# Attention's small products regrouped in the first pass of a two-block kernel

## The chip, the cores and the metric

The kernel runs on one core of a Trainium2 chip. The time is device microseconds (us) of that core for one execution. Before the change the median of three runs is 789.23 us (788.98 to 789.61).

## The reference

Two blocks follow each other. The first is an attention without softmax, per batch and head; the second mixes along the sequence and then along the channels.

```python
kv = np.einsum('bhsd,bhse->bhde', k, v)            # 8 x 8 heads, seq 576, head_dim 64
out = np.einsum('bhsd,bhde->bhse', q, kv)
rms = np.sqrt(np.mean(out * out, axis=-1, keepdims=True) + 1e-06)
x = out / rms * g_norm                             # then (B, S, H*D) = (8, 576, 512)
h = np.maximum(x.transpose(0, 2, 1) @ w_tok1, 0.0) @ w_tok2     # 576 -> 256 -> 576
u = x + h.transpose(0, 2, 1)
result = u + np.maximum(u @ w_ch1, 0.0) @ w_ch2    # 512 -> 1536 -> 512
```

All is float32.

## The kernel before

The kernel has two passes. The first does attention and the mixing along the sequence; the second, from 193.8 us on, does the channel part. Only the first is changed.

The first pass takes the eight batches in four pairs. While one pair is mixed, the next one's attention is computed. So there are five stages, each a list of strings: `start` (attention of pair 0), `middle` (attention of pair 1, mixing of pair 0), two `steady` lists (attention of pair 2 and 3, mixing of pair 1 and 2), and `last` (mixing of pair 3). `play` (L1192) walks through a list and calls the step of each name. Every step emits its instructions at once, and all of them are kept in program order, so the lists are the order of the work on each engine and each queue. A name with a minus sign takes the step from the attention of the pair before. A digit means so many steps of the weight conversion that VectorE and ScalarE do on the side for the second pass.

The steps, with `s` the batch of the pair, `c` a tile pair of 256 sequence rows (0 and 1 of the first batch, 2 and 3 of the second; 4 holds the 64 remaining rows of both), and `t` or `h` a half:

- `kv{s}{h}` (L364): k times v for four heads, 20 matrix products that fill 64 of the array's columns; into a PSUM bank of pool `kv`, two banks. `e{s}{h}` (L379): ScalarE copies them to SBUF (`kvp`).
- `a{c}` (L404, and L418 for `a4`): q times kv, 32 products (16 for `a4`) of 64×64, four of them side by side in the array; into two PSUM banks of pool `o`, which has two.
- `g{c}{h}` (L435): VectorE multiplies a bank by the gain into the tile `x`. `q{c}{h}` (L446): ScalarE squares the bank. `t{c}{h}` (L460): VectorE sums the squares per head.
- `m`, `r`, `i` (L468, L473, L477): mean on VectorE, root on ScalarE, inverse in four VectorE instructions, once for a whole group of tiles. The groups of pairs 1 to 3 are (0, 1) and (2, 3, 4).
- `s`, `d`, `p` with a tile and a half (L493, L500, L504): scale x by the inverse, on ScalarE (eight instructions), VectorE (one) or GpSimd (one).
- `h{s}{t}` (L532): first mixing product of a batch, half of the 256 token features, four full-array products over 512 columns. `hr` (L539): the remaining rows, 64 rows of the array, followed by four ReLU of ScalarE.
- `z{i}` (L550): ScalarE copies x of tile i into a PSUM bank as the seed of the sum. `u{i}` (L556): second mixing product, two full-array products; `u8`, the remaining rows, four products that fill 64 columns. With a seed (i = 2, 4, 6) ScalarE copies the result to x, otherwise VectorE adds it. Odd i and 8 then write x to memory on GpSimd's queue. The banks of `h`, `z` and `u` come from pool `h`, which has four, in turn.
- `x{u}{half}` (L636): four VectorE transposes of finished tiles into a free part of a weight tile, and `b{u}{half}` (L620) their transfer to memory.
- `l`, `lq`, `lr`, `f`: loads of k and v, of q, of q's remainder, of raw weights, on SyncE's queue.

Every matrix product of float32 leaves two records in the profile, so `u0` is a group of 4, `h00` of 8, `kv00` of 40, `a0` of 64, `a4` of 32, `hr` and `u8` of 8. All matrix products have the same line, L133, that of a helper; the groups are told apart by their tiles: `ps_kv`, `ps_o` and `ps_r` for attention, `ps_h` and `ps_u` for the mixing.

Of the kernel before, what the change touches and what calls it, by code (L numbers as in the profile page):

```python
# [11 lines left out]
F32 = mybir.dt.float32  # L12
# [8 lines left out]
def kernel(  # L21
# [33 lines left out]
    P = 128  # L55
    B, S, DM = k.shape
    D = g_norm.shape[0]
# [7 lines left out]
    HP = H // 2  # L65
# [12 lines left out]
    def pool(name, bufs, side="left", stack=ctx, **kw):  # L78
        return stack.enter_context(tc.tile_pool(name=name, bufs=bufs, side=side,
                                                reuse_waits="tile", **kw))  # L80
# [15 lines left out]
    ps = {n: pool(f"ps_{n}", b, "left", psums, space=bass.MemoryType.PSUM)  # L96
          for n, b in (("o", 2), ("kv", 2), ("h", 4))}
# [34 lines left out]
    def matmul(*a, **kw):  # L132
        keep(nc.tensor.matmul(*a, **kw))  # L133
# [220 lines left out]
    def attention(pair, groups):  # L354
# [47 lines left out]
                           rhs=kvp[side][:, hp], start=True, stop=True)  # L402

        def attend(c):  # L404
            o = [ps["o"].tile([P, 2, HP, D], F32, name="ps_o", tag="o") for _ in range(2)]
            side = c // 2
            for t in range(2):
                for hp in range(HP):
                    for n in range(2):
                        for h in range(2):  # L410
                            r = ds(h * D, D)
                            matmul(o[h][ds(n * HF, HF), t, hp],
                                   lhsT=qT[2 * pair + side][r, hp, ds((2 * (c % 2) + t) * P + n * HF, HF)],
                                   rhs=kvp[side][r, hp, :D], start=True, stop=True)
            for h in range(2):
                bank[c, h] = o[h].rearrange("p t k d -> p (t k) d")

        def attend_rem():  # L418
            o = [ps["o"].tile([P, HP, D], F32, name="ps_r", tag="o") for _ in range(2)]
            for hp in range(HP):  # L420
                for side in range(2):
                    for h in range(2):
                        r = ds(h * D, D)
                        matmul(o[h][ds(side * HF, HF), hp], lhsT=q_rest[2 * pair + side][r, hp],
                               rhs=kvp[side][r, hp, :D], start=True, stop=True)
            for h in range(2):
                bank[4, h] = o[h]
# [86 lines left out]
        for c in range(5):  # L514
            if whole:
                steps |= {f"a{c}{t}": do(attend_tile, c, t) if c < 4 else attend_tile_rem
                          for t in range(parts(c))}
            else:
                steps[f"a{c}"] = do(attend, c) if c < 4 else attend_rem
            for h in range(parts(c)):  # L520
                steps |= {f"{n}{c}{h}": do(f, c, h) for n, f in zip("gqt", (gain, square, total))}
            for t in range(1 if c == 4 else 2):
                steps |= {f"{n}{c}{t}": do(f, c, t) for n, f in zip("spd", (scale, scale_pool, scale_vector))}
# [668 lines left out]
    def play(lines, after={}, **stages):  # L1192

        for name in " ".join(lines).split():
            if name.isdigit():
                for _ in range(int(name)):
                    next(stages["rounding"], lambda: None)()
            elif name[0] == "-":  # L1200
                stages["before"][name[1:]]()
            else:
                next(stages[s][name] for s in ("attention", "mixing", "more")
                     if name in stages.get(s, ()))()
# [28 lines left out]
    for block in tok1[2:] + tok2:  # L1233
# [11 lines left out]
        "h010 t21 m2 r2", "a30 g30 q30 i2 p20", "a31 g31 q31 t30", "h011 t31 m3 r3 p21", "a40 i3 p30 g40 q40 p31",  # L1245
        "h012 h013 t40 m4 r4 w21 i4 s40 lq0 l10 l11 lr0 lr1"]
    middle = [
        "kv00 e00 w31 w22 w23 w24", "h10 -lq1 w32 w33 w34", "kv01 e01 w41 w42",
        "h11 w43 w44", "hr l00", "a0 q00 g01 q01 g00 t00 t01", "u0 z2 f0", "u1 l01",
        "a1 q10 g11 q11 g10 t10 t11 m0 r0 lq0", "u2 i0", "kv10 e10 z4 d00", "u3 s01", "kv11 e11",  # L1250
        "u4 z6 f1", "a2 q20 g21 q21 g20 s10", "u5 t20 t21 f2", "a4 q40 g41 q41 g40 lr0 lr1 1", "u6 t40 t41 1 l10",
        "a3 q30 g31 q31 g30 lq1 d11", "u7 t30 t31 m2 r2 1 i2 p20 p21 s30", "u8 1 l11 d31"]
    steady = [[
        "kv00 kv01 e00 e01 1 -d40 f3", "h00 1 x00", "h01 1 f4 b00", "a0 q00 g01 q01 g00 l00 1",
        "h10 t00 t01 1 x01", "h11 l01 1 x10 b01", "hr 1 x11 z2 f5 f6", "a1 q10 g11 q11 g10 lq0", "kv10 kv11 e10 e11 t10 t11 m0 r0",
        "u0 i0 1", "u1 1 d00 l10", "u2 s01 z4 1 f7", "a2 q20 g21 q21 g20", "u3 s10 t20 t21",
        "u4 z6 l11", "a4 q40 g41 q41 g40 lr0 lr1 1", "u5 d11 t40 t41 1", "a3 q30 g31 q31 g30 lq1",
        "u6 t30 t31 m2 r2 i2 d20 p21 s30", "u7 1 d31 1", "u8 1 b10 b11"], [
        "kv00 kv01 e00 e01 1 -d40 f8", "h00 1 x20", "h01 1 f9", "a0 q00 g01 q01 g00",
        "h10 t00 t01 1 x21", "h11 1", "hr 1 z2 f10", "a1 q10 g11 q11 g10", "kv10 kv11 e10 e11 t10 t11 m0 r0",  # L1260
        "u0 i0 1", "u1 1 d00 f11", "u2 s01 z4 1", "a2 q20 g21 q21 g20", "u3 s10 t20 t21",
        "u4 z6 1 f12", "a4 q40 g41 q41 g40", "u5 d11 t40 t41 1", "a3 q30 g31 q31 g30",
        "u6 t30 t31 m2 r2 i2 d20 p21 s30", "u7 1 d31 b20 b21", "u8 f13"]]

    attentions = [attention(0, ((0,), (1,), (2,), (3,), (4,)))]
    attentions += [attention(p, ((0, 1), (2, 3, 4))) for p in range(1, B // 2)]

    mixings = [token_mixing(p, (2, 4, 6)) for p in range(B // 2 - 1)]
    mixings.append(token_mixing(B // 2 - 1, range(2, 9), (0, 1)))
# [15 lines left out]
    play(middle, attention=attentions[1], mixing=mixings[0], before=attentions[0],  # L1285
         more=more, rounding=rounding)
    for n in range(1, B // 2 - 1):
        play(steady[n - 1], attention=attentions[n + 1], mixing=mixings[n], before=attentions[n],
             more=more, rounding=rounding)


# [5 lines left out]
    for i in range(2):  # L1297
# [2 lines left out]
    woven = fill[0][:4] + fill[1] + fill[0][4:]  # L1300

    last = [
        "h00 2 -d40 2 o0", "h01 2 o1", "h10 2 o3", "h11 2 o2", "hr z2 1 o4", "u0 z3 1 c0", "u1 z4 1 c1 o5", "u2 z5 c2",
        "u3 z6 1 c3 o6", "u4 z7 1", "u5 z8 1", "u6 1 s0", "u7 s1 s2", "u8 s3 s4"]
    parts1 = [f for o in ORDER1 for f in split(1, o)]
    more = {f"c{i}": f for i, f in enumerate(t_sums(lambda n: uT[0][:, SB[n]]))}
# [97 lines left out]
```

## Time and profile before

| | |
|---|---|
| median of three runs | 789.23 us |
| the profiled execution's own time | 788.88 us |
| its span | 787.1 us |
| TensorE busy | 774.4 us, 98% |
| VectorE busy | 612.9 us, 78% |
| ScalarE busy | 265.4 us, 34% |
| GpSimd busy | 78.3 us, 10% |
| middle | 39.79 to 76.41 us |
| first steady stage | 76.41 to 119.21 us |
| second steady stage | 119.21 to 162.11 us |
| last stage | 162.11 to 193.76 us |

The stages are read from the starts of their first matrix products. In a row of the profile, PE is TensorE, DVE VectorE, ACT ScalarE, POOL GpSimd, SP SyncE. A row of the listing in order of time has the start, the length, engine, line, operation, output and input tiles, the shape and how many were merged; in brackets, idle time before it and what ended it. The ends of matrix products are modelled, so the text takes differences of starts.

### The profile page before, as it was taken

The page shows a single profiled execution, that of the slowest core. Times are in us where ns is not written, and L with a number is a line of the kernel's source. Part 1 is how long each engine was busy: PE and PEld are TensorE (multiplying, and loading weights), DVE is VectorE, ACT ScalarE, POOL GpSimd, SP SyncE. Part 2 cuts the span into 40 slices and gives each one's busy share as a digit, 9 for nine tenths or more (in the row PEclk, how much of TensorE's full clock was granted, in tenths as well). Part 3 has the DMA queues.
Part 4 walks back from the last instruction along what each step waited for, and adds up shares of the span by engine and source line. Part 5 has one row for each costly group of instructions (what it writes and reads, how often), then busy time and mean ns, then how long its engine had stood idle before and what let it go on. Part 6 is the DMA issues. An engine that isn't in the chain of part 4 may idle for free.

```text
span 787.1 us, 14853 instructions
## 1 busy us (share of the span) xinstructions
PE 774.4 (98%) x5832; PEld 652.6 (83%) x5832; DVE 612.9 (78%) x906; ACT 265.4 (34%) x513; POOL 78.3 (10%) x91
## 2 busy tenths in 40 slices
PE   6999999999999999999999999999999999999998
PEld 5655555544888888999988899998889999889998
DVE  2666887796776868988778889776898885787977
ACT  2356564846110133511133242123352113325211
POOL 1211212122410000010100001010000101000111
PEclk9999999999999999999999999999999999999999
DMA  9999999587699795599897579889559889655864
GB/s 295 327 334 371 361 371 344 212 268 282 235 292 337 269 339 148 154 309 205 246 236 231 151 218 272 247 203 290 148 158 283 206 222 230 200 153 151 200 173 91
DMA packets 132614, 192.12 MB, mean 244 GB/s; under 512 B 13633, under 2 KB 92225, under 8 KB 132545
## 3 DMA queue, kind: packets, MB, share of 16 engines
q1 hardware_dynamic: 115984, 167.54, 68.1%
q0 software_dynamic: 14656, 22.02, 13.7%
q10 hardware_dynamic: 1904, 1.61, 0.7%
q8 instruction: 46, 0.75, 0.4%
q14 instruction: 24, 0.19, 0.1%
HBM read 138.31 MB, written 52.82 MB: 243 GB/s over the span
## 4 chain that ended last, share of the span: by engine, by line
PE 95%; DVE 2%; ACT 1%; DMA 1%; issue 0%; SPq 0%; ACTq 0%
PE ps_d L133 28%; PE ps_b L133 19%; PE ps_a L133 19%; PE ps_h L133 8%; PE ps_u L133 8%; PE ps_v L133 5%; PE ps_c L133 3%; PE ps_kv L133 2%; PE ps_w L133 2%; PE ps_o L133 2%; DMA raw<-in_moe_w_tok_dram 1%; ACT x L498 1%; DVE x L444 0%; DVE ms L465 0%; PE ps_j L133 0%
## 5 line engine op out<-in xcount | busy, mean ns | idle before, releaser
L133 PE MATMUL ps_d<-ui,w 128*128 128x256 f32 x504 | 118.6, 379 | 0.0
L133 PEld LDWEIGHTS ps_d<-ui,w 128*128 128x128 f32 x504 | 95.1, 190 | 12.8 <-DVE v L124 0.2
L130 ACT COPY ps_d<-ps_a 128x768 f32<-128x768 f32 (+1 forms) x56 | 32.0, 571 | 215.6 <-PE ps_a L133 215.6
L124 DVE TENSOR_TENSOR v<-v,v 128x1536 f32<-128x1536 f32 (+2 forms) x70 | 103.5, 1483 | 0.3
L133 PE MATMUL ps_b<-w,sv 128*128 128x128 f32 x672 | 84.7, 276 | 0.0
L133 PE MATMUL ps_a<-w,v 128*128 128x128 f32 x672 | 84.2, 275 | 0.0
L133 PEld LDWEIGHTS ps_a<-w,v 128*128 128x128 f32 x672 | 79.9, 192 | 0.2
L133 PEld LDWEIGHTS ps_b<-w,sv 128*128 128x128 f32 x672 | 79.5, 192 | 0.2
L133 PE MATMUL ps_u<-h,w_tok 128*128 128x512 f32 (+1 forms) x160 | 67.2, 606 | 0.2
L133 PE MATMUL ps_d<-w,v 128*128 128x128 f32 x528 | 66.3, 275 | 0.0
L133 PE MATMUL ps_h<-x,w_tok 128*128 128x512 f32 (+1 forms) x160 | 65.5, 603 | 0.7 <-ACT x L498 0.7
L133 PEld LDWEIGHTS ps_d<-w,v 128*128 128x128 f32 x528 | 62.7, 192 | 0.3
L127 ACT ACTIVATE v<-v 128x768 f32<-128x768 f32 (+1 forms) x54 | 42.6, 821 | 55.1 <-DVE v L124 55.1
L133 PE MATMUL ps_d<-w,sv 128*128 128x128 f32 x480 | 60.1, 275 | 0.0
L133 PEld LDWEIGHTS ps_d<-w,sv 128*128 128x128 f32 x480 | 57.1, 192 | 0.2
L133 PEld LDWEIGHTS ps_h<-x,w_tok 128*128 128x128 f32 (+1 forms) x160 | 26.1, 189 | 32.7 <-issue 29.0
L1121 POOL DMA_DIRECT2D out_dram<-us x11 | 14.1, 1278 | 379.3 <-ACT us L130 347.4
L133 PEld LDWEIGHTS ps_u<-h,w_tok 128*128 128x128 f32 (+1 forms) x160 | 24.8, 179 | 31.0 <-issue 25.6
L133 PE MATMUL ps_a<-uT,w 128*128 128x256 f32 x192 | 46.7, 379 | 0.0
L444 DVE TENSOR_TENSOR x<-ps_o,g_sb 128x512 f32<-128x512 f32 x32 | 21.6, 687 | 28.6 <-PE ps_o L133 23.3
L133 PE MATMUL ps_b<-ui,w 128*128 128x256 f32 x168 | 40.8, 379 | 0.0
L133 PEld LDWEIGHTS ps_a<-uT,w 128*128 128x128 f32 x192 | 36.3, 190 | 4.8
(145 smaller groups left out, 1216.2 us busy)
## 6 DMA issues: line engine op xcount, KB each, us to landing
w<-parts SPq DMA_DIRECT2D x168, 384.0 KB, 4.1
w<-parts SPq DMA_DIRECT2D x56, 192.0 KB, 3.4
uT<-blocks SPq DMA_DIRECT2D x36, 256.0 KB, 5.7
k_in<-in_k_dram SPq DMA_DIRECT2D x16, 512.0 KB, 8.7
qT<-in_q_dram SPq DMA_DIRECT2D x8, 1024.0 KB, 9.2
out_dram<-x POOLq DMA_DIRECT2D x16, 512.0 KB, 6.1
v_in<-in_v_dram SPq DMA_DIRECT2D x14, 512.0 KB, 8.8
raw<-in_moe_w_ch_dram SPq DMA_DIRECT2D x8, 768.0 KB, 10.4
```

What stands on the lines that cost most here:

```text
L124: keep(engine.tensor_tensor(out=o, in0=a, in1=b, op=op))
L127: keep(nc.scalar.activation(o, a, AF.Relu))
L130: keep(nc.scalar.copy(o, a))
L133: keep(nc.tensor.matmul(*a, **kw))
L444: keep(nc.vector.tensor_mul(x, bank[c, h], g_sb.to_broadcast([P, number(c), D])))
L498: keep(nc.scalar.activation(x[:, k, h], x[:, k, h], AF.Copy, scale=inv[:, k, h]))
L1121: keep(nc.gpsimd.dma_start(to.rearrange("t p e -> p t e"), a, accum_op=ALU.add))
```

## The change

- `a0` and `a4` put their results into the banks of pool `kv` instead of pool `o`.
- `a3` with all that follows it (its squares, gains, sums, `d31`, `s30`) goes to the start of the next stage, and so do `u8` and the load `lq1`. In the second steady stage `a3` and `u8` stand at the end, and `i3`, `d31`, `s30` in the last stage.
- The groups of the statistics become (0, 1), (2, 4) and (3,).
- Within the stages kv steps stand side by side, `a3` with `a0`, `a2` with `a4`; in `middle` also `a0` with `a1`. Seeds (`z`), transposes (`x`) and conversion steps are put at other places in the lists.

```diff
         def attend(c):
-            o = [ps["o"].tile([P, 2, HP, D], F32, name="ps_o", tag="o") for _ in range(2)]
+            n = "o" if c else "kv"
+            o = [ps[n].tile([P, 2, HP, D], F32, name="ps_o", tag=n) for _ in range(2)]
...
         def attend_rem():
-            o = [ps["o"].tile([P, HP, D], F32, name="ps_r", tag="o") for _ in range(2)]
+            o = [ps["kv"].tile([P, HP, D], F32, name="ps_r", tag="kv") for _ in range(2)]
...
     middle = [
-        "kv00 e00 w31 w22 w23 w24", "h10 -lq1 w32 w33 w34", "kv01 e01 w41 w42",
-        "h11 w43 w44", "hr l00", "a0 q00 g01 q01 g00 t00 t01", "u0 z2 f0", "u1 l01",
-        "a1 q10 g11 q11 g10 t10 t11 m0 r0 lq0", "u2 i0", "kv10 e10 z4 d00", "u3 s01", "kv11 e11",
-        "u4 z6 f1", "a2 q20 g21 q21 g20 s10", "u5 t20 t21 f2", "a4 q40 g41 q41 g40 lr0 lr1 1", "u6 t40 t41 1 l10",
-        "a3 q30 g31 q31 g30 lq1 d11", "u7 t30 t31 m2 r2 1 i2 p20 p21 s30", "u8 1 l11 d31"]
+        "kv00 kv01 e00 e01 w31 w22 w23 w24", "h10 -lq1 w32 w33 w34", "h11 w41 w42 w43 w44", "hr l00",
+        "a0 q00 g01 q01 g00 t00 t01", "a1 q10 g11 q11 g10 t10 t11 m0 r0 l01 lq0", "u0 z2 f0", "u1 z4 i0 d00",
+        "u2 s01", "kv10 kv11 e10 e11 x00", "u3 s10 d11 f1", "u4 z6 l10", "a2 q20 g21 q21 g20",
+        "a4 q40 t20 g41 q41 t21 g40 lr0 lr1 1", "u5 t40 t41 m2 r2 f2", "u6 1 i2 p20 p21 l11", "u7 1 1"]
     steady = [[
-        "kv00 kv01 e00 e01 1 -d40 f3", "h00 1 x00", "h01 1 f4 b00", "a0 q00 g01 q01 g00 l00 1",
-        "h10 t00 t01 1 x01", "h11 l01 1 x10 b01", "hr 1 x11 z2 f5 f6", "a1 q10 g11 q11 g10 lq0", "kv10 kv11 e10 e11 t10 t11 m0 r0",
-        "u0 i0 1", "u1 1 d00 l10", "u2 s01 z4 1 f7", "a2 q20 g21 q21 g20", "u3 s10 t20 t21",
-        "u4 z6 l11", "a4 q40 g41 q41 g40 lr0 lr1 1", "u5 d11 t40 t41 1", "a3 q30 g31 q31 g30 lq1",
-        "u6 t30 t31 m2 r2 i2 d20 p21 s30", "u7 1 d31 1", "u8 1 b10 b11"], [
...
+        "kv00 kv01 e00 e01 -d40 f3", "-u8", "-a3 -q30 -g31 -q31 -g30 -t30 -t31 -m3 -r3",
+        "a0 q00 g01 q01 g00 -i3 -d31 -s30 t00 t01 -lq1 l00", "h00 b00 1 1", "h01 f4 x01 1", "h10 1 l01 b01 x10",
+        "h11 1 x11 1", "hr z2 f5 f6", "a1 q10 g11 q11 g10 lq0", "kv10 kv11 e10 e11 t10 t11 m0 r0", "u0 i0 1",
+        "u1 z4 1 d00 l10", "u2 s01 1 f7", "a2 q20 g21 q21 g20", "a4 q40 t20 g41 q41 t21 g40 lr0 lr1", "u3 s10 l11",
+        "u4 z6 t40 t41 m2 r2 d11", "u5 1 i2 d20 p21 1", "u6 1 x20", "u7 1 1 b10 b11"], [
+        "kv00 kv01 e00 e01 -d40 f8", "-u8", "-a3 -q30 -g31 -q31 -g30 -t30 -t31 -m3 -r3",
+        "a0 q00 g01 q01 g00 -i3 -d31 -s30 t00 t01 -lq1", "h00 1 1", "h01 f9 x21 1", "h10 1", "h11 1 1", "hr z2 f10",
+        "a1 q10 g11 q11 g10", "kv10 kv11 e10 e11 t10 t11 m0 r0", "u0 i0 1", "u1 z4 1 d00 f11", "u2 s01 1",
+        "a2 q20 g21 q21 g20", "a4 q40 t20 g41 q41 t21 g40", "u3 s10", "u4 z6 t40 t41 m2 r2 d11 1 f12",
+        "u5 1 i2 d20 p21", "u6 1 b20 b21", "u7", "a3 q30 g31 q31 g30", "u8 t30 t31 m3 r3 f13"]]
...
-    attentions += [attention(p, ((0, 1), (2, 3, 4))) for p in range(1, B // 2)]
+    attentions += [attention(p, ((0, 1), (2, 4), (3,))) for p in range(1, B // 2)]
...
-        play(steady[n - 1], attention=attentions[n + 1], mixing=mixings[n], before=attentions[n],
+        play(steady[n - 1], attention=attentions[n + 1], mixing=mixings[n], before=attentions[n] | {"u8": mixings[n - 1]["u8"]},
...
-        "h00 2 -d40 2 o0", "h01 2 o1", "h10 2 o3", "h11 2 o2", "hr z2 1 o4", "u0 z3 1 c0", "u1 z4 1 c1 o5", "u2 z5 c2",
+        "h00 -i3 -d31 -s30 2 -d40 2 o0", "h01 2 o1", "h10 2 o3", "h11 2 o2", "hr z2 1 o4", "u0 z3 1 c0", "u1 z4 1 c1 o5", "u2 z5 c2",
```

The second steady list of before is the first with other loads, transposes and transfers; it ends with "u7 1 d31 b20 b21", "u8 f13".

## The prediction

> **What bounds the kernel now.** I read the page first, then TensorE in order of time, then ScalarE in order of time.
>
> ```profile
> PE 774.4 (98%) x5832; PEld 652.6 (83%) x5832; DVE 612.9 (78%) x906; ACT 265.4 (34%) x513; POOL 78.3 (10%) x91
> ...
> PE 95%; DVE 2%; ACT 1%; DMA 1%; issue 0%; SPq 0%; ACTq 0%
> ```
>
> TensorE is busy 98% of the span and 95% of the chain that ended last. So a microsecond put into or taken out of TensorE's order moves the end by a microsecond, as long as nobody else becomes late. Next, TensorE in order of time (start, length with modelled end, group; I use differences of starts):
>
> ```profile
> 52.69 3.70 PE L133 MATMUL ps_u<-h,w_tok 128*128 128x512 f32 x8
> 56.32 1.16 PE L133 MATMUL ps_o<-kvp,qT 64*64 64x64 f32 x64
> 57.41 1.98 PE L133 MATMUL ps_u<-h,w_tok 128*128 128x512 f32 x4
> 59.33 1.39 PE L133 MATMUL ps_kv<-v_in,k_in 128*64 128x64 f32 x40
> 60.64 1.98 PE L133 MATMUL ps_u<-h,w_tok 128*128 128x512 f32 x4
> ...
> 97.07 2.55 PE L133 MATMUL ps_kv<-v_in,k_in 128*64 128x64 f32 x80
> 99.55 5.42 PE L133 MATMUL ps_u<-h,w_tok 128*128 128x512 f32 x12
> 104.90 1.16 PE L133 MATMUL ps_o<-kvp,qT 64*64 64x64 f32 x64
> 105.99 4.09 PE L133 MATMUL ps_u<-h,w_tok 128*128 128x512 f32 x8
> 110.01 0.69 PE L133 MATMUL ps_r<-kvp,qR 64*64 64x64 f32 x32
> ```
>
> Full-array runs of 4, 8 and 12 records between tiled ones take 1.91, 3.63 and 5.35: 0.4293 per record plus 0.197, the price of the two edges. One kv step takes 1.31, two side by side 2.48, not 2.63; so a kv step is 1.166 plus edges of 0.05 in and 0.10 out. An attention step takes 1.09 = 0.933 + 0.159, the remainder 0.62 = 0.466 + 0.159. The run of 8 at 105.99 takes 4.02 against 3.63: u4 waited 0.39 there, 0.28 until its seed was in the bank and 0.10 for starting again. ScalarE in the same stretch shows why, and what the change will meet:
>
> ```profile
> 105.06 0.58 ACT L130 COPY x<-ps_u 128x512 f32<-128x512 f32 x1 [2.42 <-PE ps_u L133]
> 105.54 2.02 ACT L498 ACTIVATE x<-x,inv 128x64 f32<-128x64 f32 x8
> 107.46 0.58 ACT L130 COPY ps_u<-x 128x512 f32<-128x512 f32 x1
> 107.98 1.06 ACT L448 ACTIVATE sq<-ps_o 128x512 f32<-128x512 f32 x2
> 108.94 2.01 ACT L498 ACTIVATE x<-x,inv 128x64 f32<-128x64 f32 x8
> 110.85 0.57 ACT L130 COPY x<-ps_u 128x512 f32<-128x512 f32 x1
> 111.31 0.59 ACT L130 COPY ps_u<-x 128x512 f32<-128x512 f32 x1
> ```
>
> ScalarE runs gapless from copying u2 out (105.06), through s01, z4, the squares of tile 2 and s10, to copying u4 out and seeding z6 (111.31), in just the order of the step lists. TensorE's u4 waits for z4 in that queue.
>
> **The skill.** "TensorEngine Tiling (Array Packing)", Key Properties: changing the tiling mode, not just the tile, drains TensorE. The trace agrees: an edge costs 0.05 to 0.10, two products of one form none. "TensorE: Matmul & The Clock Gate", the section on the 16 sub-arrays: ScalarE and VectorE take their queues strictly in order. The listing agrees; my waits rest on this. "PSUM — Partial Sum Buffer", the section on bank collisions: two engines may not use one bank at once, two readers included. Here the square of the second bank starts only after its gain (58.36 after 57.58+0.69).
>
> **The edges.** From middle's first kv product at 39.79 to the last stage's first product at 162.11 are 122.32 us. Tiled with the prices above, the new order without any wait is:
>
> - middle: kv kv 2.48, h10 h11 7.07, hr 1.92, a0 a1 2.03, u0–u2 5.35, kv kv 2.48, u3 u4 3.63, a2 a4 1.56, u5–u7 5.35: 31.87.
> - first steady stage: kv kv 2.38, u8 1.82 (the same form as kv, so one edge less), a3 a0 2.03, h00–h11 13.93, hr 1.92, a1 1.09, kv kv 2.48, u0–u2 5.35, a2 a4 1.56, u3–u7 8.78: 41.34.
> - second: the same, a3 1.09 and u8 1.87 at its end: 44.30.
>
> Sum 117.51, which is 4.81 less. Of this 1.43 are waits of before that go: a3 for the o bank (0.31 at 71.64, 0.17 and 0.18 inside the later a3) and u4 for z4 (0.385 twice). The edges proper give 3.38.
>
> **New wait in middle, at u2.** z2 now stands behind the whole of tile 1, r0 (the square root) included; r0 needs m0, which needs t11. Tensor order: u0 starts 53.28, so u2 is wanted at 53.28+0.10+8×0.4293 = 56.82. hr ends at 51.25; in before the last relu ended 1.67 after hr, so 52.93 here. q00 then runs 52.86–53.46, and VectorE steps on at its usual spacing (0.6 each): g00 53.49, t00 54.10, t01 54.69, g11 55.28, g10 55.89, t10 56.49, t11 57.08–57.76, m0 to 57.97, r0 58.00–58.24, z2 58.14–58.75. With 0.05 to TensorE, u2 starts 58.80: 1.98 late, 2.08 with the restart. Behind r0 on ScalarE only z2 and z4 wait.
>
> **New wait in both steady stages, at u6.** z4 moves up and is on time. z6 still follows u4, but a2 and a4 now go before u3, so all their squares stand ahead of it while TensorE has no attention left to spend time on. From u2's end, T: copy u2 T+0.25, s01 +0.73 (8 at 0.239 = 1.92), q20 +2.66, g20 after it +3.29, t20 +3.90, g41 +4.50–4.91, q41 +5.00, s10 +5.27 (1.92), copy u4 +7.19, z6 +7.66–8.24, u6 +8.30. TensorE wants u6 at T + 1.65 (a2 a4) + 5.26 (u3–u5) = T+6.91: 1.39 late, 1.49 with the restart.
> In the second stage the conversion count puts the ScalarE half of a block between s01 and q20: 18 conversion steps are done before the stage, six more by h11, and u0, u1, u2 bring the 25th to 27th; the 27th starts channel block 9, of the 1024 form (1.15+1.12, some 2.07 in a row). All behind it shifts by that: 3.46, with restart 3.56.
>
> **What else moves.** A third group of statistics: mean, root and inverse for c=3, some 1.05 us of VectorE and 0.23 of ScalarE per pair (by the 16-column rows near 39.5: 0.18, 0.25, 0.18, 0.18, 0.25 and 0.22). a3's squares, sums, d31 and s30 and u8's add go to the next stage's start. h10 needs s30 at its third product, 15.1 us into the stage; a3 ends at 5.1, then g31, g30, t30, t31, m3, r3, g01, g00, i3 bring s30 to its end at about 13.0. Two microseconds of cover; a later s30 would be paid one to one. POOL's u8 stores (0.58, 0.60, 0.55) move with u8, and its X buffer is wanted by g40 only 25 us later. lq1 (1 MB, 9.2 to landing) passes SP's f3 or f8 and follows a3; a2 wants it 25 us on. It costs nothing unless 15 late, and blocks b10, b11 come free of the wait they had behind it. x00 (1.4 of VectorE) enters middle, x20 the first steady stage; VectorE was busy 23.72 of 36.60 in middle, so the gaps carry it. kv10 finds a0's banks free 6 us earlier. In the last stage t30, t31, m3, i3, d31 are new on VectorE, 3.1 us; it stood idle 7.21 before ps_v, so they fit.
> An unseen quantity is the edge from kv's 128×64 form to 64×64 through u8; taken like others at 0.15, its bounds are the smallest edge seen, 0.05, and a whole pair of them, 0.35, so −0.2 to +0.4 over the two stages.
> After 162 TensorE shows no wait over 0.11 us, so the shift goes through to the end.
>
> **Sum.** −3.38 −1.43 +2.08 +1.49 +3.56 = +2.3 us. Against the profiled execution's own 788.88 (span 787.1) this gives 791.2; the median is 0.35 above it, so I predict 791.5. A measurement here tells about 0.2%, 1.6 us, from no change.
>
> **Rivals.**
>
> 1. *Smaller waits, within 0.2%.* If block 9's conversion does not fall ahead of q20, the second stage waits like the first: 2.3−2.07 = +0.2, 789.5. For it: conversion steps may slip when VectorE is late. Against: both queues are written out in order, so the conversion can only slip as a whole. 0.22.
> 2. *Faster: no wait at z6.* If ScalarE reaches z6 before u5 ends, the 1.49 and 3.56 vanish and 5.05 less gives 786.4. The place is the stretch copy u2 to z6; it decides if this stretch is 1.4 shorter in one stage and 3.5 in the other. Against: 0.239 per scale and 0.5 per square are in every row. 0.08.
> 3. *Slower still: h10 waits for s30.* VectorE beside POOL's scaling is slow: the conversion's last step took 1.48 instead of 0.92 at 163.54, and "SBUF — State Buffer", Who interferes with whom, describes such blocking. If that and a late raw block eat the two microseconds of cover and one more in each stage, +2 gives 793.5. 0.12.
>
> My forecast has 0.58, its own range 790.6 to 792.3. Faster: rival 2 and a sliver, 0.09. Within: rival 1 with the low end of the forecast, 0.24. Slower: 0.67. The range reaches over rival 1 and most of rival 3: 789.2 to 793.4.
>
> **What would show it.** Right: ps_u waits near 56.8 for 2 us until a seed copy that follows a root; one near 111.7 of about 1.4 and one near 154.4 of about 3.5, each ended by a seed copy; first product of the last stage at about 164.4 instead of 162.11; kv and attention groups starting 2.48 and 2.03 apart. Wrong: seeds copied before the root or before s10; h10 waiting for s30; waits of TensorE after 162.

## The result, and the profile after

The median rises from 789.16 us to 797.40 us (four runs each: 788.98 to 789.61 before, 795.93 to 797.78 after). The ratio is 1.0099, with a 95% interval of 1.0086 to 1.0113. The forecast of 791.5 had the direction, but only 2.3 of the 8.2 us, and its range ended at 793.4.

The head of the page and the chain that ended last, of the kernel after:

```profile
PE 774.4 (97%) x5832; PEld 653.9 (82%) x5832; DVE 616.4 (78%) x921; ACT 267.0 (34%) x516; POOL 77.9 (10%) x91
...
PE 88%; DMA 5%; DVE 2%; ACT 2%; issue 1%; SPq 1%; ACTq 0%; DVEq 0%
```

The number of products is the same, and so is TensorE's busy time, in a span of 795.2 us instead of 787.1. Nearly all of the 8.1 us more stand in the first pass. Its stages now start at 39.87 (middle), 74.19, 118.82 (steady) and 169.85 (last), and the second pass at 201.50. The last stage takes 31.65 as before. It starts 7.74 later than before, of which 0.08 were there at the start of middle. The other 0.36 of the 8.1 come in the second pass and were not looked into.

That DMA has 5% of the chain instead of the 1% of before is not 4% of lost time. Followed back, the chain leaves TensorE at the second kv step of middle, which waits 0.19 us for v, and runs through transfers and their issue from there to the start. In the kernel before, it goes through the engines in that stretch.

The list of TensorE's waits between 39 and 195 us has the names (us in total, times, longest; short waits are left out of it):

```profile
PE ps_u L133 <- ACT ps_u L130: 6.2, 3, 3.2
PE ps_o L133 <- issue: 2.8, 2, 1.5
PE ps_kv L133 <- DMA v_in<-in_v_dram: 0.2, 1, 0.2
```

The first row was forecast: three groups of products (u2, and u6 twice) that wait for a seed which ScalarE copies into PSUM. The other two were not. In the second row, "issue" says that TensorE waited for nothing that the profile shows. TensorE in order of time gives the places:

```profile
53.76 3.70 PE L133 MATMUL ps_u<-h,w_tok 128*128 128x512 f32 x8
59.26 1.98 PE L133 MATMUL ps_u<-h,w_tok 128*128 128x512 f32 x4 [1.79 <-ACT ps_u L130]
...
78.39 2.09 PE L133 MATMUL ps_o<-kvp,qT 64*64 64x64 f32 x126
81.98 0.33 PE L133 MATMUL ps_o<-kvp,qT 64*64 64x64 f32 x2 [1.51 <-issue]
...
108.57 5.42 PE L133 MATMUL ps_u<-h,w_tok 128*128 128x512 f32 x12
115.19 3.70 PE L133 MATMUL ps_u<-h,w_tok 128*128 128x512 f32 x8 [1.20 <-ACT ps_u L130]
...
123.02 1.74 PE L133 MATMUL ps_o<-kvp,qT 64*64 64x64 f32 x103
126.06 0.58 PE L133 MATMUL ps_o<-kvp,qT 64*64 64x64 f32 x25 [1.31 <-issue]
...
152.90 5.42 PE L133 MATMUL ps_u<-h,w_tok 128*128 128x512 f32 x12
161.56 5.40 PE L133 MATMUL ps_u<-h,w_tok 128*128 128x512 f32 x8 [3.24 <-ACT ps_u L130]
```

- u0 to u2 take 7.41 instead of 5.35: u2's wait, +2.06. u3 to u7 of the first steady stage take 10.25 instead of 8.78: u6's wait, +1.47.
- a3 and a0 side by side take 3.85 and 3.56 instead of 2.03. TensorE stops two records (one product) before the end of a0 in one stage and 25 records before it in the other, in the middle of a group whose other products run.
- In the second steady stage u3 to u7 take 13.99. The wait before u6 is 3.51 of the surplus. The rest follows it: u6 and u7 start 5.33 before the next group, where eight such records otherwise take 3.63. That is 1.70 more, and the row's 5.40 against 3.70 in the first stage shows it too.

The view of stretches has what TensorE was given in that one (stretch, length, busy time of TensorE, its weight loads, VectorE, ScalarE and GpSimd, granted clock, DMA share, GB/s):

```profile
161.60:166.90 5.30, 5.30 (x10) 2.00 (x10) 4.94 (x9) 1.85 (x4) 2.28 (x2) 0.68 0.82 247
```

The granted clock is 0.68 on average here and 1.00 in the stretch before. Taken more finely, it is 0.50 from 161.92 to 165.33, so for 3.41 us, and 1.00 around that. The records in it come 0.85 us apart instead of 0.43; half of 3.41 are the 1.70 that were lost.

ScalarE in order of time shows both kinds of seed as the prediction has them, z2 behind the root and z6 behind squares and scaling:

```profile
58.49 0.23 ACT L476 ACTIVATE root<-ms 128x32 f32<-128x32 f32 x1 [1.34 <-DVE ms L471]
58.62 1.09 ACT L130 COPY ps_u<-x 128x512 f32<-128x512 f32 x2
...
153.91 1.11 ACT L163 ACTIVATE w_ch<-raw 128x1024 f32<-128x1024 f32 x1
154.93 1.13 ACT L166 ACTIVATE raw<-raw 128x1024 uint32<-128x1024 uint32 x1
155.96 1.05 ACT L449 ACTIVATE sq<-ps_o 128x512 f32<-128x512 f32 x2
...
158.55 2.01 ACT L499 ACTIVATE x<-x,inv 128x64 f32<-128x64 f32 x8
160.46 0.57 ACT L130 COPY x<-ps_u 128x512 f32<-128x512 f32 x1
160.93 0.59 ACT L130 COPY ps_u<-x 128x512 f32<-128x512 f32 x1
```

Put together, from starts of matrix products (us, in the profiled execution):

| term | forecast | measured |
|---|---|---|
| edges | −3.38 | −3.38 |
| waits of before that go | −1.43 | −1.43 |
| u2 waits for z2 | +2.08 | +2.06 |
| u6 waits for z6, first steady stage | +1.49 | +1.47 |
| u6 waits for z6, second steady stage | +3.56 | +3.51 |
| u6 and u7 after it at a lower clock | 0 | +1.70 |
| pauses between a3 and the end of a0 | 0 | +1.83, +1.53 |
| kv01 waits for v | 0 | +0.41 |
| start of middle | 0 | +0.08 |
| sum, to the last stage | +2.3 | +7.8 (7.74 by the stage starts) |

### The profile page after: what moved, and what is told of

It reads as the page before. It is cut to its first block, busy times and chain, and to the rows that moved or that the text cites. A ratio compares the mean times of both kernels' runs of the same rounds, so it can differ in the third digit from the quotient of the medians.

```text
span 795.2 us, 14874 instructions
## 1 busy us (share of the span) xinstructions
PE 774.4 (97%) x5832; PEld 653.9 (82%) x5832; DVE 616.4 (78%) x921; ACT 267.0 (34%) x516; POOL 77.9 (10%) x91
## 4 chain that ended last, share of the span: by engine, by line
PE 88%; DMA 5%; DVE 2%; ACT 2%; issue 1%; SPq 1%; ACTq 0%; DVEq 0%
PE ps_d L133 27%; PE ps_b L133 18%; PE ps_a L133 18%; PE ps_h L133 7%; PE ps_u L133 7%; PE ps_v L133 5%; DMA v_in<-in_v_dram 3%; PE ps_c L133 3%; PE ps_w L133 2%; PE ps_kv L133 2%; PE ps_o L133 1%; ACT x L499 1%; DMA raw<-in_moe_w_tok_dram 1%; SPq L121 1%; DMA xt<-out_dram 1%
```

## The theory and its rivals

What had to be explained were the pauses in a3–a0 (3.36) and the lower clock (1.70).

**Instructions.** The trace lists TensorE's instruction queue among the DMA queues: 46 packets, 0.75 MB, 16.3 KB each. TensorE leaves 5832 records of products and as many of weight loads, some 254 per packet. In the stretch from 79 to 82.5 us the view of transfers has exactly one such packet:

```profile
q8 instruction: 1, 0.02, 1.8%
```

The trace has it from 79.79 to 80.77; TensorE goes on at 81.98. The second starts at 123.75, and TensorE goes on at 126.06. Counted over TensorE's records, the two pauses stand before instruction 1985 and 3009, which are 1024 or four times 256 apart. So it looks as if instructions come in blocks of 256, one per packet, and TensorE gets to the end of a block before the next one is there. kv kv u8 a3 a0 are 160 + 16 + 256 = 432 instructions in 6.2 us; the block before 1985 would have been done in 2.82 us. In the kernel before, the shortest block of the first pass from middle on lasts 7.95. "Runtime: NRT & Kernel Launch", Instruction fetch mechanics, in the Trainium skill has the same sizes: blocks of 16 KiB, 256 instructions, the next one fetched while the current one runs. It calls the cost mostly hidden; at these two places it isn't, and the measurement decides.

The rival: a0 or a3 waits for a bank, for q or for kv in a way that the profile doesn't name.

**The clock.** "TensorE: Matmul & The Clock Gate", What's actually happening, says that the array falls to half its rate after an idle window of about 3.4 us. The gap between two records was 3.84 us here. After u2's wait, a gap of 2.39, there was nothing of the kind. The rival: what the records read or what runs beside them makes them slow.

## The experiments

All times are medians; the kernel before stood between 788.95 and 789.18 in the four groups of runs.

### z2 ahead of tile 1

```diff
-        "a0 q00 g01 q01 g00 t00 t01", "a1 q10 ... m0 r0 l01 lq0", "u0 z2 f0", ...
+        "a0 q00 g01 q01 g00 z2 t00 t01", "a1 q10 ... m0 r0 l01 lq0", "u0 f0", ...
```

> In the middle stage the seed z2 follows a0's square of the first bank instead of tile 1's root. Theory: u2's pause of 2.06 us in the middle stage is nothing but the seed's place in ScalarE's queue; the pause goes, TensorE is 2.06 us earlier from there on, 797.2 - 2.06 = 795.1. Rival: u2 waits for something else too (the PSUM bank that the seed goes into, the shared x), then the pause stays near 2 us and the time within 0.5 us of 797.2.

Measured: 795.08 (791.47 to 797.20). ScalarE in order of time copies the seed 4.8 us earlier than in the kernel after, directly behind a0's squares:

```profile
52.89 1.09 ACT L449 ACTIVATE sq<-ps_o 128x512 f32<-128x512 f32 x2
53.86 0.61 ACT L130 COPY ps_u<-x 128x512 f32<-128x512 f32 x1
```

u0 to u2 take 5.35 again, and the first steady stage starts 2.38 earlier (2.06 from u2, most of the rest from v's wait, which isn't there in this execution). The rival falls. The median agrees less well than it looks, for the runs spread over 5.7 us: in the profiled one, of 797.20, a lower clock also follows the first a3–a0 pause (2.04 here) and costs 1.70 us, and the one behind z6 lasts longer (6.83 us, which cost 3.08 instead of 1.70).

### z6 ahead of s01

```diff
-        ... "u2 s01 1 f7", ... "u4 z6 t40 t41 m2 r2 d11", ...
+        ... "u2 z6 s01 1 f7", ... "u4 t40 t41 m2 r2 d11", ...
```

The second steady list has the same edit.

> In both steady stages the seed z6 follows u2 instead of u4. Theory: the pauses at u6 (1.47 us in the first stage, 3.46 in the second) come from z6 standing behind the squares, s10 and, in the second, block 9's conversion; and the 1.7 us by which the products after the second pause run long come from that pause. All go: -1.47 -3.46 -1.7 = -6.7, about 790.5. Rival: the products after u6 run slowly for a reason of their own; then 1.7 of it stays, about 792.2. Second rival: u6 is late because of u4's copy out or the bank, then the pauses stay and the time is near 797.

Measured: 791.28 (790.81 to 793.98), 6.1 less. u6 waits no more, and no record after it is slow. As the edit takes both away together, it doesn't tell whether the wait made the records slow; the experiment that keeps TensorE busy in the wait does. The median is 0.8 above the 790.5 expected. Two waits are new, which together are more than that: u7 of the second stage waits 0.5 for VectorE, and h10 in the last stage 0.63 for s30. In the profiled execution (the slowest of these) the first a3–a0 pause was followed by a lower clock, which cost 1.70 us.

### h00 between a3 and a0

```diff
-        "a0 q00 g01 q01 g00 -i3 -d31 -s30 t00 t01 -lq1 l00", "h00 b00 1 1", ...
+        "h00 b00 -i3 -d31 -s30 1 1", "a0 q00 g01 q01 g00 t00 t01 -lq1 l00", ...
```

Both steady lists.

> In both steady stages h00 (eight records of full-array products) is put between a3 and a0. Theory: the pauses inside a3-a0 (1.83 and 1.53 us) come from TensorE running out of instructions, since kv kv u8 a3 a0 are 432 instructions in 6.4 us; with 3.4 us of large products in between a page of 256 instructions lasts longer and both pauses go: -3.36 plus two more pairs of edges at 0.2 each and a0's pair 0.16 each, about -2.7, 794.5. Rival: a3 or a0 waits for data or a bank that the profile doesn't name; then the pause goes with the group that has it and the time rises by the edges, +0.7, about 797.9.

Measured: 794.09 (793.42 to 796.18). TensorE in order of time:

```profile
78.11 1.16 PE L133 MATMUL ps_o<-kvp,qT 64*64 64x64 f32 x64
79.20 3.70 PE L133 MATMUL ps_h<-x,w_tok 128*128 128x512 f32 x8
82.83 1.16 PE L133 MATMUL ps_o<-kvp,qT 64*64 64x64 f32 x64
```

a3 takes 1.09, a0 takes 1.09, in both stages, and "issue" is gone from the waits. The two further changes of form cost 0.36 per stage. But a0 also stands later here, by 3.6 us: something that comes late would be there by then. So this alone does not exclude the rival.

### Block 9's conversion later

```diff
-        ... "u2 s01 1", ... "u4 z6 t40 t41 m2 r2 d11 1 f12", "u5 1 i2 d20 p21", "u6 1 b20 b21", "u7", ...
+        ... "u2 s01", ... "u4 z6 t40 t41 m2 r2 d11 1", "u5 1 i2 d20 p21 f12", "u6 1 b20 b21", "u7 1", ...
```

Second steady list only.

> In the second steady stage the conversion step that starts block 9 is moved from u2 to u7. Theory: the pause at u6 shrinks from 3.4 to 1.4 us, as in the first stage (-2.07), and the products after it run at full rate, since only a pause as long as 3.4 us lets TensorE fall to a lower rate (-1.7): 797.2 - 3.8 = 793.4. Rival: the slow products are not from the pause's length; only -2.07, 795.1. Second rival: the conversion isn't what made the second pause longer; no change.

Measured: 793.62 (793.10 to 794.43). TensorE in order of time:

```profile
153.03 5.42 PE L133 MATMUL ps_u<-h,w_tok 128*128 128x512 f32 x12
159.65 3.70 PE L133 MATMUL ps_u<-h,w_tok 128*128 128x512 f32 x8 [1.20 <-ACT ps_u L130]
```

The wait is that of the first stage, and u6 and u7 take 3.63. Both parts of the 3.8 us come out: u3 to u7 take 10.25 instead of 13.99, which is 2.04 of conversion and 1.70 of clock.

### More products in the start stage

```diff
-        "kv00 e00 l00 j14 w01 ...", "kv01 j10 e01 l01",
+        "kv00 e00 l00 j14 w01 ...", "kv01 j52 e01 l01",
```

The 42 products are of the identity with itself, and nobody reads them. They are 168 instructions of TensorE.

> The steps of all stages stay as in the kernel after; only in the start stage 42 more products of the identity (128x128, unused, 168 instructions of TensorE) run before the first mixing. With them the boundary between two blocks of 256 instructions that fell into a0's last products falls some 168 instructions earlier in the work, at about the first kv product of the stage. Theory (instructions are fetched in blocks of 256 and the next one isn't there yet): both pauses inside a3-a0, 1.83 and 1.53 us, vanish or move to another place, at most one or two others appear where a block is dense; the start stage is longer by about 4 to 5 us. Rival (a0 or a3 waits for data or a bank): the pauses stay inside a3-a0 with the same lengths, only later by the longer start stage.

Measured: 802.42 (802.26 to 803.02). The start stage is 9.46 longer, not 4 to 5: a product of float32 leaves two records, 0.112 us each, which the expectation counted once. The first steady stage:

```profile
83.25 2.55 PE L133 MATMUL ps_kv<-v_in,k_in 128*64 128x64 f32 x80
85.63 1.89 PE L133 MATMUL ps_u<-h,w_tok 128*64 128x512 f32 x8
87.45 2.10 PE L133 MATMUL ps_o<-kvp,qT 64*64 64x64 f32 x128
```

a3 and a0 take 2.03 in both stages, without a pause. The order of work in all stages from middle on is the same, and so is each wait for a seed (2.07, 1.47, and 3.5 with the lower clock behind it); only where the count of instructions stands is another. That excludes the rival: a bank or a tile that a0 needs would be late here too. A transfer that comes at a fixed time would be on time here, but the pauses keep no fixed time: with z2 ahead of tile 1 the first ends at 79.87 instead of 81.98, and its packet starts at 77.29 instead of 79.79.

The run also shows that a block with little work in it need not end in a pause. By the same count, the boundary before instruction 1985 now falls into a3, at 88.08, after a block of 4.7 us, and a block from 105.33 to 108.27 has 2.9 us. Neither has a pause at its end. The last packet before 88.08 had started at 82.11, some six us ahead; in the kernel after it started 2.2 us before TensorE could go on. So, by these figures, what counts is how early the next block's packet starts, and not the density alone.

### Only the banks, in the kernel before

```diff
-            o = [ps["o"].tile([P, 2, HP, D], F32, name="ps_o", tag="o") for _ in range(2)]
+            n = "o" if c else "kv"
+            o = [ps[n].tile([P, 2, HP, D], F32, name="ps_o", tag=n) for _ in range(2)]
```

`a4` likewise; the order of before.

> The kernel before with only a0 and a4 in the banks of pool kv, the order unchanged. Theory: a3 and the other groups no longer wait for an o bank, 0.31 + 0.17 + 0.18 = 0.66 less, 788.3 against 788.95; the rest is as before, since kv steps find their banks free long before. Rival: kv10 or the copies of kv then wait for a0's squares, and nothing is gained or up to 1 us is lost.

Measured: 788.53 against 789.18, a ratio of 0.9993 with an interval of 0.9985 to 1.0001. The stages are 0.30, 0.18 and 0.17 shorter in the profile, which is the size expected; the times can't tell it from nothing.

### All three repairs

z2 ahead of tile 1, z6 ahead of s01, h00 between a3 and a0: the edits of the first three experiments.

> The kernel after with z2 behind a0's first square, z6 behind u2 in both steady stages, and h00 between a3 and a0. Theory: the three seeds' pauses, the pauses for instructions and the products at half rate all go, the edges and the waits that the change removed stay removed: 797.2 - 2.06 - 6.7 - 2.65 = 785.8, which is 3.2 below the kernel before (the edges' 3.38 and the waits' 1.43, less 0.71 for two more excursions, less up to 0.4 for v in the middle stage: -3.7). Rival: a saved pause turns into another one, since VectorE and ScalarE have the same work in less time; then 787 to 790.

Measured: 787.39 (786.03 to 789.10) against 789.18; the ratio is 0.9974, 0.9967 to 0.9981. It is 0.26% faster than before, but 1.6 above the expectation, and the rival has a share in it. TensorE's waits from 39 to 195 us:

```profile
PE ps_r L133 <- issue: 0.4, 1, 0.4
PE ps_h L133 <- ACT x L499: 0.4, 1, 0.4
PE ps_u L133 <- DVE x L124: 0.2, 1, 0.2
```

In differences of starts these are 0.68, 0.63 and 0.50. The first is a block of instructions again, in the a2–a4 group of middle, before instruction 1473, which is 512 ahead of the old place. The second is the wait for s30 that the prediction held against h10 as its third rival: three conversion instructions of VectorE, 3.4 us, stand ahead of a3's gains. The third is VectorE's add of u3, queued behind g20, which waits for q20, which waits for block 9's conversion. While TensorE still stood waiting elsewhere, both had time.

### The conversion moved as well

This starts from the kernel of the experiment before.

```diff
-        ... "u2 z6 s01 1", ... "u4 t40 t41 m2 r2 d11 1 f12", "u5 1 i2 d20 p21", "u6 1 b20 b21", ...
+        ... "u2 z6 s01", ... "u4 t40 t41 m2 r2 d11 1", "u5 1 i2 d20 p21 f12", "u6 b20 b21", ...
...
-        ... "h01 2 o1", "h10 2 o3", ...
+        ... "h01 3 o1", "h10 3 o3", ...
```

> The kernel of the experiment before (all three repairs), with one conversion step less at u2 and one less at u6 of the second steady stage, and one more each at h01 and h10 of the last stage. Theory: the 0.4 us that u7 waits for VectorE's add of u3 in the second steady stage (block 9's conversion stands ahead of q20, and the gains, then the add, behind q20) and the 0.52 us that h10 waits for s30 in the last stage (three conversion instructions of VectorE, 3.4 us, stand ahead of a3's gains) both go: 787.39 - 0.9 = 786.5. Rival: the conversion that is put off makes another reader late in the last stage; then 787.4 or more.

Measured: 785.26 (784.41 to 786.62) against 789.06; the ratio is 0.9954, 0.9942 to 0.9967. It beats both kernels, and is 1.2 below the 786.5 expected. The list of TensorE's waits from 38 to 195 us is empty, and u3 to u7 of the second steady stage are one run:

```profile
145.97 8.85 PE L133 MATMUL ps_u<-h,w_tok 128*128 128x512 f32 x20
```

From middle's first product to the last stage's first are 118.33 us. The prediction's sum without waits, 117.51, and two more pairs of changes of form, 0.71, make 118.22; the other 0.11 are about what a short pause in the a2–a4 group of middle costs, 0.13. So the edges and the banks are worth what they were said to be, once nothing waits.

### TensorE kept busy in the long wait

```diff
+    def keep_busy():
+        o = ps["o"].tile([P, 2, HP, D], F32, name="ps_j", tag="o")
+        for _ in range(14):
+            matmul(o[:, :, 0, :], lhsT=ident, rhs=ident, start=True, stop=True)
...
-        "u5 1 i2 d20 p21", "u6 1 b20 b21", "u7", ...
+        "u5 1 i2 d20 p21", "jo", "u6 1 b20 b21", "u7", ...
```

The kernel after, second steady list only; nobody reads these products.

> The kernel after with 14 unused products of the identity between u5 and u6 of the second steady stage, which need some 3.1 us of TensorE and no data, so that it works through most of the pause in which it waits for z6. Theory (TensorE runs at half rate because it stood still for 3.4 us): u6 starts at the same time after u5 as before, since z6 comes no earlier, but the records after it come 0.43 apart again, -1.7, 795.5. Rival (the records are slow for what they read or what the other engines do there): they stay at 0.85 and the time at 797.2. Second rival: the products end after z6 has come, then u6 is up to 0.5 later.

Measured: 795.01 (794.12 to 796.28). TensorE in order of time:

```profile
152.17 5.42 PE L133 MATMUL ps_u<-h,w_tok 128*128 128x512 f32 x12
157.43 3.29 PE L133 MATMUL ps_j<-ident 128*128 128x128 f32 x28
160.82 3.70 PE L133 MATMUL ps_u<-h,w_tok 128*128 128x512 f32 x8
```

u6 starts 8.65 after u3, in the kernel after 8.66: z6 comes no earlier. But u6 and u7 take 3.63 again, not 5.33. Useless work in a wait made the kernel faster by 2.4, of which the profile shows 1.70 at this place. So the low clock at u6 comes from TensorE's standing still, and not from what u6 reads or from what the other engines do there.

## Why the prediction was wrong, point by point

- **Right:** what bounds the kernel; the edges, to 0.01 us per group; the waits of before that go; u2's wait (2.08 forecast, 2.06 measured); both waits at u6 with their causes, block 9 in front of q20 included; no wait of TensorE over 0.2 us from the last stage on, so that the shift goes through to within 0.36. The first two rivals of the prediction, smaller waits and no wait at z6, did not come.
- **Wrong, 3.36 us: the step "The edges".** This is the largest part of what was missed. Its sum for "the new order without any wait" took prices from short groups and set them side by side without a limit on how long such a row may be. kv kv u8 a3 a0 is a row of 432 small instructions, and TensorE runs out of them where the next block's packet starts too late (1.83 and 1.53 us). The prediction listed VectorE, ScalarE, banks and transfers as things that can be late, and not the instructions themselves. That instructions are what is late is shown by the shifted count (both pauses gone, same order); the packets' times agree.
- **Wrong, 1.70 us: the restart in "New wait in both steady stages".** It was taken at 0.10 for any wait, from a wait of 0.28. After the wait of 3.4 it was 1.80. The mechanism of the wait was right, its aftermath was not sized. The page on the clock gate, which the prediction cites for something else, states this fall.
- **Wrong, 0.41 us: "What else moves".** kv01 starts 3.6 us earlier in middle, and its v was not looked at. It cost 0 to 0.46 in the executions profiled.
- **The third rival, too early.** h10 did not wait for s30 in the kernel after, whose pauses gave VectorE time. It did so by 0.63 as soon as the waits for z6 were gone, in the last stage, while the rival had reckoned the cover in the steady stages. One reading there mixed two forms: the conversion step of 1.48 at 163.54 has 2048 elements, and that form takes 1.22 at 186.75, not 0.92. Of the form with 1536 elements, the step beside GpSimd's scaling takes 1.50 (79.64) and one without 0.91 (85.40), so the effect is real.

Two things stay open. One is why a block's packet starts where it does: 1.8 to 3.1 us after TensorE crossed the boundary before it in the rows with a pause, but 1.25 ahead of it in the first stage of the run with more products. The other is most of the spread between runs of one kernel. A part of it is the lower clock: of the kernel after, three executions have a mean clock of 0.997 or 0.998 and spans of 795.0 to 795.4 us, and one has 1.000 and 793.4.

## What to carry to other kernels

Putting small tiled products side by side saves changes of form, here up to 0.36 us a time, but it also thickens the stream of instructions: count those of the densest row. By these runs, a block of 256 that would be done in less than about 6 us (an estimate: blocks of 2.4 to 3.9 and of 6.1 to 6.2 us ended in pauses here, others as short did not) can stop TensorE, depending on where the boundaries fall; large products in between helped. Moving matrix work away from other engines' work takes away the time in which those engines produced its seeds, so when a group moves, walk the queue of whoever feeds the next one. And price a wait with its aftermath: behind the gap of 3.84 us, the lower clock cost 1.7 us or more.

## What the runs showed of the hardware

- **When the next block of instructions can be used.** In the ten a3–a0 pauses of five kernels TensorE went on 2.2 to 2.6 us after the block's packet started, though the packet itself took 0.9 to 1.1. The blocks that ended in these pauses took 4.4 to 5.4 us instead of 2.4 to 3.9. Small pauses, of 0.1 to 0.7, were seen in the a2–a4 group of middle, after blocks that would have taken 6.1 to 6.2.
- **The lower clock** is 0.50 for 3.41 us, or for twice that. In the kernel after it begins 0.36 us after TensorE went on. It came at each gap of 3.84 us that stood idle in the four profiled executions that have one, with 1.7 to 3.1 us lost, and after none of the gaps of 1.8 and 2.4 within full-array products. But it isn't certain: of the 16 executions of these four kernels, profiled or not, four have a mean clock of 1.000, where one such stretch would give 0.998. It also came after two of the a3–a0 pauses, both of 2.0 us, and not after the eight others, of 1.0 to 1.9, in the same two groups. Why it follows a pause of 2.0 there and not the gap of 2.4 elsewhere, no run tested.
